# A new hand-written order of 914 operations, with new PSUM banks, in a one-core S4 mixer and MLP kernel

## The chip, the core and the metric

The kernel runs on one core of a Trainium2 chip. The metric is the device time of one execution in microseconds (us); lower is better. The engines are PE (TensorE, matrix multiplication), ACT (ScalarE), DVE (VectorE), POOL (GpSimd) and SP (SyncE, which here only issues transfers). "PEld" in the profile is PE's weight load.

## The reference

Two blocks with a residual each, over a sequence of 2048 rows of 512 channels in bfloat16:

```python
def A(u):                      # S4 convolution: N = 128 complex states for each channel
    dt = exp(log_dt)[:, None]
    logdA, dB = dt * (A_re + 1j * A_im), dt * (B_re + 1j * B_im)
    P = exp(logdA[:, :, None] * arange(L))
    K = einsum("dn,dnl,dn->dl", C_re + 1j * C_im, P, dB).real
    y = irfft(rfft(pad(u.T)) * rfft(pad(K)))[:, :L].T
    return y + u * Dskip
def B(x):                      # 512 -> 1376 -> 512
    return gelu(layernorm(x) @ w1 + b1) @ w2 + b2
h = x + A(layernorm(x))
out = h + B(layernorm(h))
```

The norms have no scale and no shift; the GELU is the tanh form. What a chip sees of part A is mostly the making of K (exponentials, sines, and chains of them), transforms written as matrix products, and the products of spectra.

## The kernel before

All work is recorded first, as 914 operations. `add(eng, cost, fn, r, w, new)` notes which engines may run an operation (one, or a choice of two), what it reads and writes, and which new PSUM tiles it opens. `Sched.run` then issues the operations strictly in the order of a list written out by hand:

```python
given = iter(SLOTS)
for k in ORDER:
    if k < 0:                    # a filler: four identity matmuls into bank -1-k, L1451
        ...
    o = ops[k // 2]
    o.e = o.eng[k % 2]           # which of its engines runs it
    for p in o.new:
        p.slot = int(next(given))  # which PSUM bank the tile takes
    order.append(o)
```

So an entry 2n is operation n on its first engine, 2n+1 the same operation on its second, and each engine gets its part of the list as its queue. `SLOTS` is a string of 196 digits, one bank of eight for each new PSUM tile. An engine never runs ahead of its own queue, and a matmul into a bank waits until what was there has been read.

The work in the order of time, with the lines in the profile of before:

- Kernel generation. Exponentials on ACT (L793), exponentials of the phases (L991, from matmuls at L988), then two chains of sines. The B chain has matmuls L1013/L1018, sines L1026 on ACT, multiplications L1036/L1043 on DVE. The A chain (chain1) has matmuls L1058/L1061, sines L1063 and multiplications L1068. It needs rows that go through DRAM (HL_d) and back. K is then made on PE (L1092), and its spectrum (L1120, L1145, L1166, L1187).
- Transforms of the normalised input: L946, L967, L971.
- The inverse, `inverse`, for two halves (b = 0, 1) and four chunks of channels. Each has two multiplications on DVE (L1235, 128x2048) or, for the last chunk, L1210, L689 and L1225; then matmuls (L1245), an evacuation of the bank, and a turn: on PE for one chunk (L1254), with a transposing transfer (L1261) for the others.
- `tail`: per quarter of the rows, matmuls L1315/L1319, the residual (L1322, or L1315 in the first), row statistics (L1323 and small DVE operations at L689 and L694), the normalised copy y2 (L1334 on DVE, L1336 on ACT), transposes on PE (L1346) in the first quarter and a transposing transfer in the others.
- `mlp`: for each quarter eleven groups of four matmuls (L1362) with a GELU on ACT (L1364), then matmuls L1378, the second residual L1380 on DVE, and stores.

`evac` copies a PSUM tile to SBUF, on ACT (L616) or on DVE (L618). `table` loads an activation table on ACT (L610). `dma` issues a transfer from SP or ACT (L632).

Of the kernel before, what the change touches and what calls it, by code (L numbers as in the profile page):

```python
# [275 lines left out]
class VS(V):  # L276
# [13 lines left out]
LAG = {"PE": 0.12, "ACT": 0.20, "DVE": 0.14, "POOL": 0.15, "SP": 0.15}  # L290
OWN = {"PE": 0.0, "ACT": 0.17, "DVE": 0.11, "POOL": 0.1, "SP": 0.0}
ORDER = [
# [35 lines left out]
]  # L328
SLOTS = "0124624620462046042642640426420206464620242002606204206242604026462064202064026406246024602406206420642016240364710404160364160743104523712460453347247364163210657000423751452706341725310671620547"


TURN = 450000
# [2 lines left out]
class Sched:  # L335
# [54 lines left out]
    def run(self, nslots):  # L390
# [13 lines left out]
        taken = [None] * nslots  # L404
        given = iter(SLOTS)
        order, seen = [], set()
# [1094 lines left out]
```

## Time and profile before

| | |
|---|---|
| median of three executions | 228.2 us (228.09 to 228.47) |
| profiled execution: span, first to last instruction | 226.4 us |
| granted TensorE clock, mean | 0.997 |
| PE busy | 198.1 us (87%), 2989 instructions |
| PE weight loads | 112.4 us (50%) |
| DVE busy | 174.3 us (77%) |
| ACT busy | 164.9 us (73%) |
| POOL busy | 13.8 us (6%) |

The profiled execution has no time of its own beside the span; the span lies 1.8 us below the median of the three. The shares are averages over stages with different limits, so they don't say what bounds a stage; the windows and the chain of waits do.

### The profile page before, as it was taken

Reading aid. Unit: us, or ns where it says so; the run is one execution under the profiler, and the core shown is the slowest. Engines: PE = TensorE matmul, PEld = TensorE weight load, DVE = VectorE, ACT = ScalarE, POOL = GpSimd, SP = SyncE. Lnnn points to the kernel's source line nnn. Section 1 sums busy time; section 2 is a strip of 40 time slices with the busy share of each in tenths; the row PEclk is TensorE's granted clock in tenths of the full one; section 3 lists DMA queues with packets and bytes.
Section 4 is the critical chain, followed back from the end, with each engine's and each line's share of the span. In section 5 each row is a group of like instructions: output and inputs, shape, how many; then the busy total and the mean of one; then the engine's idle time right before and its main releaser. Section 6 shows DMA issues by size and latency. Waiting matters only on the chain.

```text
span 226.4 us, 6876 instructions
## 1 busy us (share of the span) xinstructions
PE 198.1 (87%) x2989; PEld 112.4 (50%) x2989; DVE 174.3 (77%) x277; ACT 164.9 (73%) x205; POOL 13.8 (6%) x26
## 2 busy tenths in 40 slices
PE   6314977768999999999999868999999999999993
PEld 3102743234767478566576556644443444444552
DVE  7999789999998898889999999899827476013022
ACT  4999999999988998989999469695156206801900
POOL 2000301200010003000000010300000101000000
PEclk9999999999999999999999999999999999999998
DMA  5992074250003964657789495383050131313202
GB/s 152 179 189 74 7 243 128 50 146 6 6 3 75 130 174 135 163 143 213 163 176 280 136 306 110 108 191 90 0 127 0 32 88 46 72 44 78 75 23 70
DMA packets 43159, 25.09 MB, mean 111 GB/s; under 512 B 30197, under 2 KB 40697, under 8 KB 43130
## 3 DMA queue, kind: packets, MB, share of 16 engines
q1 hardware_dynamic: 42968, 24.59, 45.2%
q8 instruction: 23, 0.38, 0.7%
q10 hardware_dynamic: 162, 0.07, 0.1%
q14 instruction: 6, 0.05, 0.1%
HBM read 14.13 MB, written 5.28 MB: 86 GB/s over the span
## 4 chain that ended last, share of the span: by engine, by line
PE 65%; ACT 17%; DVE 11%; DMA 3%; issue 2%; POOL 0%; DVEq 0%; ACTq 0%; SPq 0%; POOLq 0%
PE ps L1378 17%; PE ps L1362 17%; PE ps L1092 8%; ACT ar L793 7%; PE ps L1245 6%; PE ps L946 4%; DVE ar L1235 4%; ACT ar L616 4%; PE ps L967 3%; ACT ar L1063 3%; ACT ar L991 3%; DVE ar L618 2%; DMA HL_d<-ar 2%; PE ps L1145 1%; PE ps L1061 1%
## 5 line engine op out<-in xcount | busy, mean ns | idle before, releaser
L616 ACT CAST ar<-ps 128x1024 bf16<-128x1024 f32 (+4 forms) x72 | 61.9, 903 | 14.0 <-PE ps L1245 9.2
L1364 ACT ACTIVATE ar<-ps,ar 128x512 bf16<-128x512 f32 (+1 forms) x44 | 27.0, 692 | 28.7 <-PE ps L1362 20.5
L1378 PE MATMUL ps<-ar 128*128 128x512 bf16 (+3 forms) x187 | 40.2, 367 | 0.0
L1362 PE MATMUL ps<-ar 128*128 128x512 bf16 (+1 forms) x176 | 39.8, 379 | 0.0
L1380 DVE TENSOR_TENSOR ar<-ps,ar 128x512 bf16<-128x512 f32 (+1 forms) x17 | 10.8, 655 | 28.3 <-PE ps L1378 28.3
L1378 PEld LDWEIGHTS <-ar 128*128 128x128 bf16 (+1 forms) x187 | 17.9, 98 | 19.7 <-issue 0.7
L1362 PEld LDWEIGHTS <-ar 128*128 128x128 bf16 (+1 forms) x176 | 17.3, 100 | 20.5 <-issue 0.8
L1235 DVE TENSOR_TENSOR ar<-ar 128x2048 bf16<-128x2048 bf16 x20 | 23.9, 1220 | 1.0 <-PE ps L1245 0.5
L1245 PE MATMUL ps<-ar 64*128 64x128 bf16 x672 | 21.7, 216 | 3.1 <-DVE ar L1235 2.1
L618 DVE CAST ar<-ps 128x1024 bf16<-128x1024 f32 (+3 forms) x19 | 21.3, 1129 | 3.3 <-PE ps L946 1.7
L1245 PEld LDWEIGHTS <-ar 64*128 64x128 bf16 x672 | 19.0, 94 | 7.8 <-DVE ar L1235 4.6
L1063 ACT ACTIVATE ar<-ps 128x1024 bf16<-128x1024 int16 x20 | 19.7, 1027 | 1.7 <-PE ps L1061 1.0
L1092 PE MATMUL ps<-ar 128*52 128x66 bf16 x512 | 19.4, 242 | 0.3 <-DVE ar L618 0.2
L1092 PEld LDWEIGHTS <-ar 128*52 128x52 bf16 x512 | 16.9, 130 | 4.4 <-issue 2.6
L689 POOL TENSOR_TENSOR ar<-ar 128x4 f32<-128x4 f32 (+1 forms) x6 | 8.6, 1436 | 141.7 <-DVE ar L694 99.5
L946 PE MATMUL ps<-ar 128*32 128x512 bf16 x256 | 15.9, 381 | 0.5 <-ACT ar L991 0.3
L793 ACT ACTIVATE ar<-ar 128x1024 bf16<-128x1024 f32 x16 | 15.7, 1045 | 0.6 <-DVE ar L788 0.6
L1026 ACT ACTIVATE ar<-ps 128x1024 bf16<-128x1024 int16 x16 | 15.7, 1033 | 0.3 <-PE ps L1018 0.2
L1068 DVE TENSOR_TENSOR ar<-ar 128x1024 bf16<-128x1024 bf16 x20 | 13.1, 685 | 1.2 <-ACT ar L1063 1.0
L967 PE MATMUL ps<-ar 128*64 128x512 bf16 (+2 forms) x160 | 14.0, 298 | 0.1
L1322 DVE TENSOR_TENSOR ar<-ps,ar 128x512 bf16<-128x512 f32 x12 | 8.0, 683 | 7.9 <-ACT ar L1364 4.3
L1061 PE MATMUL ps<-ar 128*32 128x256 f16 (+1 forms) x256 | 12.7, 301 | 1.2 <-ACT ar L1063 1.1
(85 smaller groups left out, 232.0 us busy)
## 6 DMA issues: line engine op xcount, KB each, us to landing
ar<-in_A_u_dram SPq DMA_DIRECT2D x16, 128.0 KB
ar<-in_A_u_dram SPq DMA_DIRECT2D x8, 256.0 KB
out_dram<-ar SPq DMA_DIRECT2D x30, 64.0 KB
ar<-in_B_w_dram SPq DMA_DIRECT2D x4, 344.0 KB
ar<-in_B_w_dram SPq DMA_DIRECT2D x2, 640.0 KB
AK_d<-ar SPq DMA_DIRECT2D x2, 512.0 KB
ar<-AK_d SPq DMA_DIRECT2D x2, 512.0 KB
AKc_d<-ar SPq DMA_DIRECT2D x4, 256.0 KB
```

What stands on the lines that cost most here:

```text
L616: act.copy(out_fn(), in_fn())
L618: dve.tensor_copy(out_fn(), in_fn())
L793: add("ACT", c_act(1024) + 0.03, lambda e, e0=e0: act.activation(free(EB0 // 2 + 4 * (16 - e0), [[8 * e0, 2], [4 * NB, NCH * CW // 4], [1, ...
L946: pe.matmul(pst(p)[32 * j:32 * j + 32, 512 * z:512 * z + 512], lhsT=BX.ap()[:, f0 + z, 16 - 16 * c:48 - 16 * c], rhs=src[2 * j + c].ap(), ...
L967: pe.matmul(pst(p)[64 * h:64 * h + 64, w * (k + r):w * (k + r) + w], lhsT=T.ap()[:, f, r, :], rhs=v[f:f + 1].ap()[:, 0, :], start=True, st ...
L1063: add("ACT", c_act(1024), lambda e, sc=sc: act.activation(sc.ap().rearrange("p z a b -> p (z a b)").rearrange("p (x a f) -> p a x f", a=4, ...
L1092: pe.matmul(o, lhsT=free(ta.lo // 2 + q * 4 * NP_ + f, [[4, NP_ + NA]]), rhs=free(tb.lo // 2 + q * 4 * NB + f, [[4, 2 * NB]]), start=ta is ...
L1235: dve.tensor_tensor(pq.ap().rearrange("p n d -> p (n d)"), a, b_, ALU.mult)
L1245: pe.matmul(pst(p)[:, 512 * h + 128 * k:512 * h + 128 * k + 128], lhsT=q.ap()[rows, x, :], rhs=TP[w].ap()[rows, f0 // 2 + k, :], start=(n ...
L1362: pe.matmul(pst(p)[:fs], lhsT=w1s[dc].ap()[:, fc * P:fc * P + fs], rhs=ybuf.ap().rearrange("p (t c) k -> p c t k", c=4)[:, dc], start=(dc ...
L1364: add("ACT", c_act(512, 1), lambda e, p=p, fc=fc, fs=fs: act.activation(hT.ap()[:fs, fc, :], pst(p)[:fs], ACT.Gelu_apprx_tanh, bias=b1_sb. ...
L1378: pe.matmul(pst(p)[:, c0:c1], lhsT=hT.ap()[:fs, fc, 128 * t:128 * t + 128], rhs=w2s[fc].ap()[:fs, c0:c1], start=(fc == 0), stop=(fc == NFC ...
```

## The change

Only the two tables at the top of the file differ. `ORDER` goes from 916 to 914 entries, `SLOTS` has the same length and other digits. The 914 operations are the same; 34 of them run on the other of their two engines. The list of before has two negative entries, -1 and -5, the fillers; the new one has none. The file gets one line longer, so that a line L1235 of before is L1236 after.

```diff
 ORDER = [
-    294, 0, 50, 2, 4, 62, 52, 154, 6, 64, 54, 8, 102, 12, 56, 66, 14, 10, 136,
+    58, 290, 0, 194, 2, 6, 52, 50, 8, 4, 54, 64, 62, 56, 10, 66, 68, 154, 102,
...
```

Three places show what the tables do. The first is ACT's queue after the table load for the sines, up to the first sine of the A chain (L1063, after L1064). L616 and L617 are evacuations. Before:

```order
L610 ACT_TABLE_LOAD
L701 ACTIVATE ar<-ar 128x512
L616 CAST ar<-ps 128x1024
L1026 ACTIVATE ar<-ps 128x1024 x6
L616 CAST ar<-ps 128x1024
L1026 ACTIVATE ar<-ps 128x1024 x2
L616 CAST ar<-ps 128x1024 x2
L1063 ACTIVATE ar<-ps 128x4x64x4 x10
```

And after:

```order
L611 ACT_TABLE_LOAD
L702 ACTIVATE ar<-ar 128x512
L1027 ACTIVATE ar<-ps 128x1024 x2
L617 CAST ar<-ps 128x1024
L1027 ACTIVATE ar<-ps 128x1024 x3
L617 CAST ar<-ps 128x1024
L1027 ACTIVATE ar<-ps 128x1024 x3
L617 CAST ar<-ps 128x1024 x3
L1064 ACTIVATE ar<-ps 128x4x64x4 x10
```

There are five evacuations among the eight sines of the B chain where there were four.

The second is DVE's queue in the first inverse chunks of the second half, where the statistics of the first quarter end (L694 behind L689) and the multiplications L1235 go on. Before:

```order
L694 SCALAR_TENSOR_TENSOR ar<-ar 128x4 x2
L1322 TENSOR_TENSOR ar<-ps,ar 128x512
L1235 TENSOR_TENSOR ar<-ar 128x2048
L694 SCALAR_TENSOR_TENSOR ar<-ar 128x4
L1235 TENSOR_TENSOR ar<-ar 128x2048
L1322 TENSOR_TENSOR ar<-ps,ar 128x512
L1323 BN_STATS ar<-ar 128x6
L1322 TENSOR_TENSOR ar<-ps,ar 128x512
L1235 TENSOR_TENSOR ar<-ar 128x2048 x2
```

And after:

```order
L690 TENSOR_TENSOR ar<-ar 128x4 x2
L695 SCALAR_TENSOR_TENSOR ar<-ar 128x4 x3
L1288 CAST ar<-ar 128x11
L1236 TENSOR_TENSOR ar<-ar 128x2048 x2
L695 SCALAR_TENSOR_TENSOR ar<-ar 128x4
L1323 TENSOR_TENSOR ar<-ps,ar 128x512
L1335 TENSOR_SCALAR ar<-ps,ar 128x512 x2
L1236 TENSOR_TENSOR ar<-ar 128x2048 x2
```

The last small operation of the statistics has moved behind the second of the two multiplications, and two scalings (L1335) have come from ACT.

The third is ACT's queue at the same place: the evacuation of an inverse tile is the one of form 128x128x8. Before:

```order
L616 CAST ar<-ps 128x128x8 x2
L1336 ACTIVATE ar<-ps,ar 128x512 x2
L616 CAST ar<-ps 128x512
L1336 ACTIVATE ar<-ps,ar 128x512
L616 CAST ar<-ps 128x512
L1336 ACTIVATE ar<-ps,ar 128x512
L616 COPY ar<-ps 128x512
L616 CAST ar<-ps 128x128x8
L616 COPY ar<-ps 128x512 x3
L616 CAST ar<-ps 128x512
L616 CAST ar<-ps 128x128x8
L610 ACT_TABLE_LOAD
```

And after:

```order
L617 CAST ar<-ps 128x4x2x128 x2
L611 ACT_TABLE_LOAD
L633 DMA ar<-in_A_u_dram 64x2048
L617 CAST ar<-ps 128x128x8
L633 DMA ar<-in_B_w_dram 128x1376 x2
L617 CAST ar<-ps 128x128x8
L1337 ACTIVATE ar<-ps,ar 128x512 x2
L617 CAST ar<-ps 128x512 x3
L617 COPY ar<-ps 128x512
L617 CAST ar<-ps 128x128x8
L617 COPY ar<-ps 128x512 x3
L633 DMA ar<-in_A_u_dram 64x2048
```

The table load for the GELU now stands ahead of the two 128x128x8 evacuations, four transfers that SP issued are issued here, two scalings are gone and the evacuations of 512 columns stand together ahead of the 128x128x8 one.

The other moves that a reader has to know, out of the 34 changes of engine: evacuations 239 and 383 of the transforms go from DVE to ACT and 389 from ACT to DVE (the first place); 233 and 241, ahead of L1120 and of the next L1120, go from DVE to ACT; 438, 463 and 466 go from DVE to ACT and 297, 300, 365 and 370 from ACT to DVE; the evacuation 510 of a turned tile goes from DVE to ACT; transfers 442, 479, 515, 517, 718 and 720 are issued by ACT and no longer by SP; a multiplication of the last chunk (697) is now some thirty operations earlier on DVE.

More of the change, by code (lines that the diff above doesn't have):

```diff
@@ L292 @@
 ORDER = [
[35 rows of a table removed]
[36 rows of a table added]
 ]
-SLOTS = "0124624620462046042642640426420206464620242002606204206242604026462064202064026406246024602406206420642016240364710404160364160743104523712460453347247364163210657000423751452706341725310671620547"
+SLOTS = "0731646240642646062424242420642004224066404662462426062400462064204626402640260246042604260246024602460230264301407644127314712531072462760513014235423170452374312767340403617410675301642056705627"
 TURN = 450000
```

71 rows, old and new, of the table ORDER are left out of this document.

## Prediction

> **What bounds the kernel now.** I read the windows first, cut where the chain of waits changes its character, then that chain, then the timelines of ACT, DVE and PE at the places where PE stands. The columns of the windows: the stretch in us from the span's start, its length, busy time of each engine (instructions), the granted TensorE clock, the share of the DMA engines, GB/s.
>
> ```profile
> core 0: us, PE busy (x) PEld busy (x) DVE busy (x) ACT busy (x) POOL busy (x), PEclk, DMA share, GB/s
> 0.00:31.00 31.00, 16.07 (x222) 10.24 (x222) 27.76 (x55) 27.90 (x32) 3.56 (x11) 1.00 0.61 135
> 31.00:56.90 25.90, 20.50 (x390) 8.95 (x386) 24.66 (x33) 25.26 (x28) 2.36 (x8) 1.00 0.35 95
> 56.90:121.30 64.40, 63.43 (x1536) 43.13 (x1536) 59.72 (x90) 59.83 (x71) 2.90 (x3) 1.00 0.58 132
> 121.30:138.40 17.10, 13.71 (x310) 9.63 (x308) 16.50 (x26) 11.99 (x16) 1.01 (x1) 1.00 0.71 202
> 138.40:222.90 84.50, 84.39 (x539) 40.46 (x539) 45.22 (x76) 39.87 (x62) 4.01 (x3) 1.00 0.31 74
> ```
>
> PE is the bound from 56.9 to 121.3 (0.97 us idle) and from 138.4 to 222.9 (0.11 us idle). Ahead of 56.9 ACT is it, with 27.90 of 31.00 and 25.26 of 25.90 us. From 121.3 to 138.4 it is DVE, 16.50 of 17.10, while PE stands for 3.39 us. So the change can act through three numbers: when the long PE stretch begins (56.89), when the last unbroken one begins (138.41), and whether either gets a hole. The chain of waits (start, us, what) says the same:
>
> ```profile
> 44.27 2.24 DMA ar<-HL_d
> ...
> 47.66 1.75 ACT ar L1063 x2
> ...
> 56.89 1.47 PE ps L1092 x40
> ...
> 71.18 1.22 DVE ar L618
> ...
> 72.56 1.96 PE ps L1120 x32
> ...
> 123.32 2.37 DVE ar L1235 x2
> ...
> 132.94 0.07 DVE ar L694
> 133.01 1.14 DVE ar L1235
> ...
> 136.07 2.29 DVE ar L1235 x2
> 138.41 1.96 PE ps L1245 x64
> ```
>
> **The change part by part.** *Fillers.* Both negative entries are gone, so PE issues eight matmuls and eight weight loads less. Timeline of PE:
>
> ```profile
> 12.95 0.40 PE L865 MATMUL ps<-ar 128*32 128x256 f16 x1 [5.09 <-DMA ar<-tab_I]
> ...
> 36.06 0.40 PE L1451 MATMUL ps<-ar 128*128 128x128 bf16 x4
> ...
> 43.49 0.38 PE L1451 MATMUL ps<-ar 128*128 128x128 bf16 x4 [0.43 <-ACT ar L616]
> ```
>
> That is 0.78 us of PE, in a stretch where PE is idle for 25.90 − 20.50 = 5.40 us and ACT sets the pace: gain 0. If ACT were not the cover, it would be 0.78 us at most. The lower bound is the clock: the row at 12.95 shows PE idle for 5.09 us, and the window 0 to 31 still has the clock at 1.00. [...]
>
> *Head, to 56.9.* ACT has, between the table load at 34.08 and the first sine of the second chain (L1063), twelve pieces of 1024 columns before (eight L1026, four evacuations) and thirteen after: evacuations 239 and 383 come from DVE, 389 goes to DVE. Timeline of ACT:
>
> ```profile
> 34.08 1.28 ACT L610 ACT_TABLE_LOAD   x1
> ...
> 45.25 1.92 ACT L616 CAST ar<-ps 128x1024 bf16<-128x1024 f32 x2
> 47.66 9.58 ACT L1063 ACTIVATE ar<-ps 128x1024 bf16<-128x1024 int16 x10 [0.48 <-PE ps L1061]
> ```
>
> One more piece takes 1.92/2 = 0.96; ACT waited 0.48 there for PE (which waited for the HL_d transfer), so the first sine moves by 0.96 − 0.48 = +0.5. Ahead of the table load the exponentials stand in another order, but their count is the same; the evacuation that leaves ACT for DVE there lets ACT start L991 no earlier than its input, so I keep 34.08. The ten sines stand behind one another in the same order, so L1092 starts at 57.4 in place of 56.89. Upper end: the whole 0.96, if the transfer is late too. Lower end: 0, since the HL_d transfer alone reached 46.51 (44.27 + 2.24).
>
> *Middle, 56.9 to 121.3.* The same PE work in another order, so only the 0.97 us of idle can change. The evacuation of 1.22 us in the chain at 71.18 (233) goes from DVE to ACT, as does 241; ACT has the cheaper one:
>
> ```profile
> L616 ACT CAST ar<-ps 128x1024 bf16<-128x1024 f32 x47 | 46.0, 1022 | 13.1 <-PE ps L1245 9.2 <-PE ps L967 1.2 <-issue 1.1
> ...
> L618 DVE CAST ar<-ps 128x1024 bf16<-128x1024 f32 x14 | 16.9, 1218 | 2.0 <-PE ps L946 1.7 <-PE ps L1120 0.3
> ```
>
> 0.2 us is the difference, and DVE is no longer asked for it there. With the other small waits I take −0.5: half of the idle, which gives back the head's delay. Ends: −0.97 (no idle left) and +1.0 (as much idle again, which the swaps in the other direction, 438, 463, 466 from DVE to ACT and 370, 365, 297, 300 from ACT to DVE, could make). Moved transfers: 479 and 442 now are issued by ACT, some 0.5 us each, where ACT has 64.40 − 59.83 = 4.57 us to spare; cover gone, they cost 1.0.
>
> *The hole, 121.3 to 138.4.* Here I find the loss. Timelines of DVE, ACT and PE:
>
> ```profile
> 122.19 0.68 DVE L618 COPY ar<-ps 128x1024 bf16<-128x1024 bf16 x1
> 123.32 2.36 DVE L1235 TENSOR_TENSOR ar<-ar 128x2048 bf16<-128x2048 bf16 x2 [0.45 <-PE ps L1245]
> ...
> 132.86 0.15 DVE L694 SCALAR_TENSOR_TENSOR ar<-ar 128x4 f32<-128x4 f32 x1
> ...
> 134.07 0.69 DVE L1322 TENSOR_TENSOR ar<-ps,ar 128x512 bf16<-128x512 f32 x1
> 134.79 0.69 DVE L1323 BATCH_NORM_STATS2 ar<-ar 128x6 f32<-128x512 bf16 x1
> ...
> 127.74 1.01 ACT L616 CAST ar<-ps 128x1024 bf16<-128x1024 f32 x1 [1.47 <-PE ps L1245]
> ...
> 132.05 1.01 ACT L616 CAST ar<-ps 128x1024 bf16<-128x1024 f32 x1 [3.29 <-PE ps L1245]
> 133.05 1.45 ACT L1336 ACTIVATE ar<-ps,ar 128x512 bf16<-128x512 f32 x2
> 134.39 0.58 ACT L616 CAST ar<-ps 128x512 bf16<-128x512 f32 x1
> ...
> 137.14 1.06 ACT L616 CAST ar<-ps 128x1024 bf16<-128x1024 f32 x1
> ...
> 141.48 1.28 ACT L610 ACT_TABLE_LOAD   x1
> 143.10 1.27 ACT L1364 ACTIVATE ar<-ps,ar 128x512 bf16<-128x512 f32 x2 [0.34 <-PE ps L1362]
> ...
> 138.41 1.96 PE L1245 MATMUL ps<-ar 64*128 64x128 bf16 x64 [0.69 <-DVE ar L1235]
> ```
>
> On DVE the copy at 122.19 (0.68) goes to ACT, and a multiplication of the last chunk (697, 1.2) takes its place and the wait of 0.45 behind it: 0.68 + 0.45 − 1.2 = +0.1. Ahead of the last two L1235 stand two scalings (540, 548; some 0.6 each, as other 512-column operations from PSUM) and no longer the L1322 at 134.07 and the L1323 at 134.79, some 0.6 each: 0. So DVE alone would reach 138.41 at +0.1.
>
> ACT has the loss. The last operation of the row statistics (539, at 132.86) stood between two L1235 and now stands behind both: 1.14, and 0.1 for a small cast put in there. So ACT's two scalings, which wait for it, start at 133.05 + 1.14 + 0.1 + 0.1 (DVE's own delay) = 134.4. Behind them ACT has two scalings (1.45), three evacuations of 512 columns (0.58 each by the row at 134.39; estimated 0.55 as one begins before the other ends) and a copy of the same size before evacuation 686, the one at 137.14 (1.06), which frees the PSUM bank of the matmuls at 138.41: 134.4 + 1.45 + 4 × 0.55 + 1.06 = 139.1. Before, 686 ended at 138.20 and DVE at 138.36. So the unbroken stretch starts at 139.15: +0.75. Ends: +0.1 (686 hidden, DVE decides) and +1.3 (the whole 1.24 of the statistics is passed on). The table load (1.28, with the 0.34 behind it) moves to ahead of the evacuation at 127.74, with a transfer's issue (718, 0.5) behind it: 2.1 us, against a wait of 1.47; 0.65 is left, and the 3.29 of waiting behind it hides that. Issues 515 and 517 (1.0) go into those 3.29 too. If nothing hid them, the upper end grows by 0.65.
>
> [...]
>
> *From the start of that stretch to the end.* Same PE work, 84.4 us, same order of halves; the last half-tile, its L1380 and its store stay last. Term 0. What gets tighter is the transposing transfer (L1261) whose result L1319 reads:
>
> ```profile
> 163.36 0.62 PE L1245 MATMUL ps<-ar 64*128 64x128 bf16 x16
> ...
> 165.23 5.34 PE L1362 MATMUL ps<-ar 128*128 128x512 bf16 x24
> 170.50 0.84 PE L1319 MATMUL ps<-ar 128*64 128x512 bf16 x6
> ...
> 165.06 1.60 SPq L1261 DMA_TRANSPOSE ar<-ar  x1
> ```
>
> From the end of L1245 (163.98) to L1319 (170.50) PE had 6.5 us of other work; now six groups of four L1362 stand between, 5.3 by the row of 24. Ends: 0 and +1.2, if all 6.5 were needed.
>
> **Sum.** 0 (fillers) + 0.5 (head) − 0.5 (middle) + 0.75 (hole) + 0 = +0.75, on a span of 226.4; the runs' median is 228.2, 1.8 above the span, and I add the change to the median: 228.95, told as 229.0. A difference of 0.2% (0.46 us) is about what a measurement of this kernel can tell from none.
>
> **Rivals.**
> 1. Faster. The swaps take the middle's idle away wholly (−0.97), the head's +0.5 doesn't appear because the HL_d transfer is the later one, and in the hole DVE decides (+0.1): 228.2 − 0.87 = 227.3. For it: the wait at 71.18 is on the chain and its evacuation got cheaper. Against it: PE has just 0.97 to give there, and 686 stands behind more of ACT's work. It decides if 686 ends before DVE's last L1235. 0.25.
> 2. No change. Middle and hole cancel (−0.5 of idle removed, head hidden, hole +0.5): 228.2. For it: PE is full for 149 of 226 us. 0.17.
> 3. More slower. The transfer at 165.06 lands late for L1319, +1.2 on the forecast's +0.75: 230.2. For it: the shorter cover. Against it: the issue ends at 166.66, 3.8 us ahead of use. 0.12.
> 4. Clock falls without the fillers. The L1092 at 56.89 would run its first 1.47 us at half speed, +1.5: 228.2 + 0.75 + 1.5 = 230.4. Against it: clock 1.00 after 5.09 us idle. 0.03.
>
> **How the numbers follow.** The forecast (about +0.5 to +1.3, 228.7 to 229.5) has 0.43. Slower: 0.43 + 0.12 + 0.03 = 0.58; same 0.17; faster 0.25. The range leaves out less than 2 in 10: down to 227.3, where the first rival ends, and up to 230.6, the sum with the hole's upper end (1.3), the head unabsorbed (0.5) and half of the third rival (0.6).
>
> **What would show it.** Head: the first L1063 at 48.1 and the first L1092 at 57.4. Middle: the L1245 at 121.39 within half a us. Hole: the scaling on ACT starting near 134.4, its 1024-column evacuation near 138.0, and the unbroken PE stretch at 139.15. Last stretch: PE idle under 0.3 us after that. I am wrong if PE's idle between 57 and 121 is not between 0.3 and 1.5, if the hole's length falls, or if a wait on a transfer or a bank opens behind 139.

## The result, and the profile after

The changed kernel takes 232.12 us (median of six, 230.03 to 234.16) beside 228.43 for the kernel before on the same chip. The ratio is 1.0122, with a 95% interval of 1.0081 to 1.0164: slower, by 2.8 us where 0.75 was forecast, and the median lies outside the range. A later series of ten gave 232.34 (228.83 to 234.00), ratio 1.0082 [1.0039, 1.0125]. The ratios leave out executions more than 1.5% above the fastest of their kernel, here one of the six (the profiled one) and five of the ten; the medians of all executions differ by 1.6 to 1.7%. The profiled execution is the slowest of the six, 234.16, with a span of 232.4. A profile of the later series (run e6 below) took 232.23; it shows the second of the two waits that follow, longer, and not the first.

The page: PE's busy time and the granted clock in 40 slices. Work is the same but for the eight filler matmuls, the idle grew, and one slice past the middle has a lower clock (the last slice lies behind PE's work).

```profile
PE 196.5 (85%) x2975; PEld 114.1 (49%) x2981; DVE 175.7 (76%) x281; ACT 162.8 (70%) x201; POOL 13.7 (6%) x26
...
PEclk9999999999999999999997999999999999999998
```

The windows, cut at the same events as before (first L1093, first L1246 of the second half's inverse, the start of PE's last unbroken stretch, its end):

```profile
56.82:126.50 69.68, 64.12 (x1538) 44.53 (x1538) 61.56 (x93) 58.97 (x69) 2.90 (x3) 0.99 0.59 132
126.50:144.83 18.33, 14.12 (x308) 10.47 (x309) 15.13 (x24) 12.67 (x17) 1.93 (x1) 0.95 0.71 187
144.83:228.70 83.87, 83.28 (x534) 40.91 (x539) 46.09 (x79) 38.07 (x59) 3.02 (x3) 1.00 0.30 66
```

The head ends at 56.82 (56.89 before). The middle is 69.68 long in place of 64.4, so PE stood for 5.6 us in place of 0.97. The next stretch is 18.33 in place of 17.1. The last is 0.6 shorter. The chain of waits says what the middle waited for, and it is transfers (start, us, what):

```profile
104.66 4.39 DMA AKc_d<-ar
...
109.98 5.03 DMA ar<-AKc_d
...
115.06 1.07 PE ps L968 x20
...
118.00 4.71 DMA ar<-ar
...
124.80 1.77 PE ps L1255 x16
```

SP issues them, and the timeline of its queue shows the reason. After (first block) and before (second), with SP's own longest wait for this write between them (us in total, times, longest):

```profile
97.94 0.41 SPq L633 DMA_DIRECT2D AL_d<-ar  x1
98.58 0.38 SPq L633 DMA_DIRECT2D AKc_d<-ar  x1
103.83 0.78 SPq L633 DMA_DIRECT2D ar<-AL_d  x1
104.66 0.46 SPq L633 DMA_DIRECT2D AKc_d<-ar  x1
...
109.12 0.34 SPq L633 DMA_DIRECT2D ar<-AKc_d  x1
...
109.98 0.43 SPq L633 DMA_DIRECT2D ar<-AKc_d  x1
110.50 4.36 SPq L1262 DMA_TRANSPOSE ar<-ar  x1
...
118.00 1.56 SPq L1262 DMA_TRANSPOSE ar<-ar  x1
...
121.36 2.84 SPq L1262 DMA_TRANSPOSE ar<-ar  x1
```

```profile
SPq L633 <- DMA AL_d<-ar: 5.9, 2, 4.7
```

```profile
96.09 2.94 SPq L632 DMA_DIRECT2D AKc_d<-ar  x2
...
104.35 0.33 SPq L632 DMA_DIRECT2D ar<-AKc_d  x1
...
106.58 2.04 SPq L1261 DMA_TRANSPOSE ar<-ar  x1
...
111.80 2.03 SPq L1261 DMA_TRANSPOSE ar<-ar  x1
...
117.30 1.58 SPq L1261 DMA_TRANSPOSE ar<-ar  x1
```

After: the load at 103.83 (operation 662) reads what the write at 97.94 (478) puts into DRAM, and SP stands for 4.7 us until that has landed. Behind it waits a write (464) that before went out at 98.67 and now goes out at 104.66. Two loads need it, the first at 109.12 when it has landed. The three transposing transfers of the first half's inverse (486, 493 and 500) stand behind them and are issued at 110.50, 118.00 and 121.36, not at 106.58, 111.80 and 117.30. The first of them also holds SP for 4.36 us, 2.04 before. PE then waits twice (timeline of PE; the row of ACT is what the second wait goes back to, the last row is before's, for the length of the same matmuls):

```profile
115.06 1.07 PE L968 MATMUL ps<-ar 128*64 128x128 bf16 x20 [1.96 <-DMA ar<-AKc_d]
...
122.81 2.84 ACT L617 CAST ar<-ps 128x1024 bf16<-128x1024 f32 x3 [2.75 <-DMA ar<-ar]
...
123.88 0.42 PE L1188 MATMUL ps<-ar 18*64 18x256 bf16 x14 [1.65 <-ACT ar L617]
...
126.50 2.84 PE L1246 MATMUL ps<-ar 64*128 64x128 bf16 x64
...
121.32 1.96 PE L1245 MATMUL ps<-ar 64*128 64x128 bf16 x64
```

The second wait is ACT's: its evacuation could not overwrite the buffer that the late transfer (118.00, 4.71 us) was still reading. The slower matmuls are a consequence of their own: these 64 took 1.96 before and take 2.84, because the clock was halved:

```profile
121.56:124.97 3.41, 1.25 (x23) 0.43 (x20) 3.41 (x5) 2.16 (x3) 0.00 (x0) 1.00 1.20 253
124.97:128.38 3.41, 3.41 (x52) 3.21 (x51) 0.62 (x2) 3.32 (x4) 0.00 (x0) 0.50 0.87 250
```

In a stretch of 3.41 us PE was busy for 1.25; in the next 3.41 us the clock is 0.50.

In the profile of e6 the waits come out otherwise. SP stands for a shorter time (662 is issued at 102.57, 464 at 103.40), and PE has no wait before L968. The transposing transfers are still issued late, at 108.57, 116.53 and 120.47, and the second wait alone makes the loss (SP, PE):

```profile
108.57 4.25 SPq L1262 DMA_TRANSPOSE ar<-ar  x1
...
116.53 2.58 SPq L1262 DMA_TRANSPOSE ar<-ar  x1
...
122.39 0.42 PE L1188 MATMUL ps<-ar 18*64 18x256 bf16 x14 [2.23 <-ACT ar L617]
```

### The profile page after: what moved, and what is told of

The parts are those of the page before. It is cut to its first block, busy times and chain, and to the rows that moved or that the text cites. A ratio compares the mean times of both kernels' runs of the same rounds, so it can differ in the third digit from the quotient of the medians.

```text
span 232.4 us, 6858 instructions
## 1 busy us (share of the span) xinstructions
PE 196.5 (85%) x2975; PEld 114.1 (49%) x2981; DVE 175.7 (76%) x281; ACT 162.8 (70%) x201; POOL 13.7 (6%) x26
## 4 chain that ended last, share of the span: by engine, by line
PE 52%; ACT 17%; DVE 15%; DMA 8%; issue 5%; SPq 2%; POOL 0%; DVEq 0%; ACTq 0%; POOLq 0%
PE ps L1363 15%; PE ps L1379 13%; PE ps L1093 6%; PE ps L1246 5%; ACT ar L617 4%; ACT ar L1064 4%; ACT ar L992 4%; DMA ar<-ar 4%; ACT ar L1027 3%; PE ps L968 3%; DVE ar L1236 2%; DMA ar<-AKc_d 2%; PE ps L947 2%; DMA AKc_d<-ar 2%; DVE ar L619 2%
## 5 line engine op out<-in xcount | busy, mean ns | idle before, releaser
L617 ACT CAST ar<-ps 128x1024 bf16<-128x1024 f32 (+3 forms) x69 | 59.6, 927 | 20.2 <-PE ps L1246 6.0
L1365 ACT ACTIVATE ar<-ps,ar 128x512 bf16<-128x512 f32 (+1 forms) x44 | 27.6, 687 | 30.9 <-PE ps L1363 30.9
L1363 PE MATMUL ps<-ar 128*128 128x512 bf16 (+1 forms) x176 | 40.1, 379 | 0.3 <-DMA ar<-ar 0.3
L1379 PE MATMUL ps<-ar 128*128 128x512 bf16 (+2 forms) x182 | 39.3, 366 | 0.3
L1363 PEld LDWEIGHTS <-ar 128*128 128x128 bf16 (+1 forms) x176 | 17.2, 100 | 20.8 <-DMA ar<-ar 0.8
L1236 DVE TENSOR_TENSOR ar<-ar 128x2048 bf16<-128x2048 bf16 x20 | 23.8, 1217 | 4.5 <-PE ps L1246 4.0
L619 DVE CAST ar<-ps 128x1024 bf16<-128x1024 f32 (+4 forms) x22 | 23.2, 1064 | 4.4 <-PE ps L947 2.0
L1246 PE MATMUL ps<-ar 64*128 64x128 bf16 x672 | 21.9, 221 | 3.6 <-DVE ar L1236 2.0
L1246 PEld LDWEIGHTS <-ar 64*128 64x128 bf16 x672 | 19.7, 97 | 7.8 <-DVE ar L1236 5.6
L1064 ACT ACTIVATE ar<-ps 128x1024 bf16<-128x1024 int16 x20 | 19.7, 1048 | 1.8 <-PE ps L1062 0.9
L1093 PE MATMUL ps<-ar 128*52 128x66 bf16 x512 | 19.0, 243 | 0.4 <-DVE ar L1069 0.4
L1093 PEld LDWEIGHTS <-ar 128*52 128x52 bf16 x512 | 17.0, 130 | 3.9 <-issue 2.0
L968 PE MATMUL ps<-ar 128*64 128x512 bf16 (+2 forms) x160 | 13.8, 298 | 3.2 <-DMA ar<-AKc_d 2.0
L690 DVE TENSOR_TENSOR ar<-ar 128x512 f32<-128x512 f32 (+3 forms) x24 | 12.2, 515 | 0.5
```

The lines of the kernel that those rows point to most:

```text
L617: act.copy(out_fn(), in_fn())
L619: dve.tensor_copy(out_fn(), in_fn())
L968: pe.matmul(pst(p)[64 * h:64 * h + 64, w * (k + r):w * (k + r) + w], lhsT=T.ap()[:, f, r, :], rhs=v[f:f + 1].ap()[:, 0, :], start=True, st ...
L1064: add("ACT", c_act(1024), lambda e, sc=sc: act.activation(sc.ap().rearrange("p z a b -> p (z a b)").rearrange("p (x a f) -> p a x f", a=4, ...
L1093: pe.matmul(o, lhsT=free(ta.lo // 2 + q * 4 * NP_ + f, [[4, NP_ + NA]]), rhs=free(tb.lo // 2 + q * 4 * NB + f, [[4, 2 * NB]]), start=ta is ...
L1236: dve.tensor_tensor(pq.ap().rearrange("p n d -> p (n d)"), a, b_, ALU.mult)
```

## The experiments

Two theories stood against the forecast's: the order on SP's queue makes transfers late ("queue"), and PE's thin stretches halve the clock ("gate"); the rival to both was that the missing fillers are the loss. Diffs show entries of the order (2n or 2n+1 is operation n). The ratio is to the kernel before, run beside them. A mean clock of 0.993 or less is counted as at least one window at half clock, an estimate from the one above (0.5 × 3.41 of some 230 us is 0.0074; the profile of before, with half clock only from 224.96 on, behind PE's work, has 0.997). It doesn't say where the window lies: five executions of e10 have means of 0.966 to 0.968, as much as four windows would take off, and took 228.01 to 228.69, no longer than the others. No profile shows where that half clock lies.

**One write moved (e1).**

```diff
-    885, 827, 750, 1324, 1260,
+    885, 827, 750, 928, 1324, 1260,
...
-    1318, 1270, 816, 928, 1274,
+    1318, 1270, 816, 1274,
```

> The changed kernel with one transfer moved: the write of a spectrum's second half (464, AKc_d<-ar) is issued by SP ahead of the load 662 (ar<-AL_d) and not behind it. Queue theory (in the changed kernel 662 waits until 103.8 for another write to land, 464 behind it is issued at 104.66 in place of 98.67, so the loads 470 and 469 that need it and the transposing transfers 486, 493, 500 come 4 to 6 us later): 464 at about 99, PE's wait of 2.0 us before L968 at 115 gone, the wait of ACT for the transposing transfer at 118 to 122.7 gone or under 1 us, granted clock 1.00 from 120 to 130; 228.5 to 229.7 us against some 231 for the changed kernel. Filler theory (the lost time is half clock for want of fillers): no change, 230 to 233. Forecast's theory (late statistics in the stretch of the second half's first inverse chunks, +0.75): no change from this edit.

Measured: 230.76 us (228.82 to 232.55), ratio 1.0061 [1.0030, 1.0092]. The wait before L968 is gone, but the transposing transfers are issued at 108.21, 114.85 and 118.31, still late by 1 to 3 us, and PE waits again, later:

```profile
121.18 0.42 PE L1188 MATMUL ps<-ar 18*64 18x256 bf16 x14 [1.20 <-ACT ar L617]
```

A window at half clock follows at 123.08 (the clock is 0.81 from 120 to 125 and 0.85 from 125 to 130, and the 64 L1246 at 123.10 take 3.56). So this write is a part of the cause; the rest counts too. The first transposing transfer is not held by the queue here: SP was free from 106.59 and waited until 108.21 for the evacuation that it reads, and e5 and e10 issue it at 108.24 and 108.17, so 1.6 us of its lateness comes from the new compute order. The second one is: four loads stand ahead of it, and SP is free only at 114.75. The time lies above what I expected.

**A load ahead of the write in the kernel before (e2).**

```diff
-    934, 933, 1260, 928,
+    934, 933, 1260, 958, 1324, 928,
```

> The kernel before with two transfers moved: the write 479 and the load 662 that waits for it stand on SP ahead of the write 464. Queue theory: SP stands for some 4 us at 662, 464 goes out near 102 to 104 in place of 98.67, the transposing transfers come some 4 us later, and PE gets a hole between 112 and 126: slower by 1 to 4 us, 229.5 to 232. Filler theory: the fillers are kept, so within 0.5 us of before. If the order of these three is not the cause, within 0.5 us of before too.

Measured: 228.50 (228.03 to 229.62), ratio 0.9998 [0.9969, 1.0026]: no loss. Here 479 is the later of the two writes that 662 reads, where in the changed kernel it is 478. It was issued at 96.63 and had landed by 98.86, so SP stood for 1.7 us and not for 4.9, and the transposing transfers came within 0.4 us of before. One pair alone does not make the loss.

**The fillers: put back (e3), taken from before (e4).**

```diff
-    298, 446, 302,
+    298, 446, -7, 302,
...
-    332, 344,
+    332, -5, 344,
```

> The changed kernel with the two fillers put back at the same operations of PE as before (four identity matmuls ahead of 151 and four ahead of 172), in banks that are free there. Queue theory: as the changed kernel, 230 to 233, with the same waits at 115 and 118 to 123. Filler theory: back to 228.2 to 229, with the clock at 1.00 between 120 and 130.

Measured: 229.98 (228.57 to 231.68), ratio 1.0060 [1.0034, 1.0086]. Not back to before, and 8 of 12 executions still had a window at half clock; but nearer to it than the changed kernel in its own series, on another chip, with intervals that overlap. In the one profile (229.03) the writes landed sooner and PE had no wait before L968, as in e6 without fillers. Its window at half clock lies in the head, from 38.68 to 42.09 (the clock is 0.93 from 31 to 57), with the fillers in place, and the first L1093 comes at 57.73. So the fillers aren't shown to help here.

```diff
-    256, -1, 490,
+    256, 490,
...
-    308, -5, 270,
+    308, 270,
```

> The kernel before without its two fillers, nothing else. Forecast's theory (the fillers stand where ACT sets the pace): within 0.3 us of before, first L1092 at 56.9. Filler theory: one more window at half clock in most executions, 0.5 to 2 us slower.

Measured: 229.39 (228.33 to 230.91), ratio 1.0024 [0.9994, 1.0054], inconclusive as a ratio; but 11 of 12 executions had a window at half clock, against 8 of 27 of the kernel before beside them (33 of 86 over three series). In the profile one of two starts at 47.43 behind a window with 1.48 us of PE, and the first L1092 comes at 57.96 and not at 56.89:

```profile
44.02:47.43 3.41, 1.48 (x28) 0.69 (x29) 3.41 (x5) 3.07 (x4) 0.00 (x0) 1.00 0.25 57
47.43:50.84 3.41, 3.15 (x48) 1.63 (x40) 3.01 (x4) 2.27 (x3) 0.00 (x0) 0.50 0.54 176
```

So the fillers make such windows rarer in the order of before. They don't keep them out: the profile of e9 below, with them and with this head, has one at 47.33 (eight L1061 take 0.65 us at 47.88, and 0.39 at 48.09 in before). In the changed order without them the clock from 31 to 57 is 1.00 in the profiles of after, e1 and e5, and the first L1093 came at 56.8 to 57.0.

**The transfers of the middle in the order of before (e5).** 718 and 720 stay on ACT.

```diff
-operations on SP: ..., 478, 468, 662, 464, 511, 470, 516, 469, 486, 663, 514, 661, 660, 493, ...
+operations on SP: ..., 478, 651, 440, 464, 442, 468, 441, 479, 511, 470, 661, 99, 486, 469, 662, 660, 493, ...
```

> The changed kernel with all transfers of SP and ACT between about 82 and 140 us (40 of them, from the writes of the first spectrum up to the second half's second transposing transfer) on SP and in the order of before; the compute engines' orders stay the new ones. Queue theory: the middle is repaired wholly, 228.3 to 229.5, the L1246 at the start of the second half's inverse near 121.4, and what is left over before is the forecast's +0.75 in the stretch 121 to 139 or less. If the compute order itself costs the time, 230 or more.

Measured: 229.95 (229.85 to 230.71), ratio 1.0065 [1.0040, 1.0089]. The spread is gone: 0.86 us in place of 4 to 5. What is left is one wait of 1.15 before L968 for 469, and a window at half clock (0.50 from 135.83 to 139.24), behind one with 1.60 us of PE:

```profile
132.42:135.83 3.41, 1.60 (x52) 1.34 (x46) 3.34 (x11) 1.01 (x1) 1.93 (x1) 1.00 1.08 287
```

All six executions had a clock of 0.990 or less, three of them 0.963. So the old order of the transfers is not by itself the repair: with the new compute order 0.65% is left.

**The changed kernel again (e6).** Unaltered.

> The changed kernel once more, unaltered, beside the others. Queue and gate theory together (loss = waits for late transposing transfers, 0 to 4 us and different from execution to execution, plus one window of 3.4 us at half clock in the stretch of the second half's first inverse chunks, 1.3 us): 229.5 to 233, every execution at a clock of 0.993 or less, and PE's last unbroken stretch 83.4 long against 84.4 before. If the first 6 executions were chance: 228.5 to 229.5.

Measured: 232.34 (228.83 to 234.00). Seven of ten had a clock of 0.993 or less, not all ten as expected; the three others took 228.83, 229.11 and 231.68. PE's last stretch is 83.38 long (143.32 to 226.70). So the first series was no accident, and the loss differs from execution to execution.

**Fillers where PE waits (e8).** On e5:

```diff
-    1362,
+    -6, -6, 1362,
...
-    1370,
+    -6, -6, 1370,
```

> The changed kernel with all transfers in the order of before (as in the earlier run with that edit alone, 229.95), and 16 identity matmuls as fillers: eight ahead of the matmuls of 681 and eight ahead of those of 685, where PE waited 0.92 and 1.46 us. Gate theory (PE's waits in that stretch make a window of too little work, and the clock is halved for the 3.41 us behind it): no window at half clock between 120 and 145, the stretch from 672 to 690 some 17.5 in place of 18.8 long, 228.5 to 229.2. If the half clock comes from elsewhere: 229.8 to 230.5, the fillers costing up to 0.6.

Measured: 229.52 (228.81 to 231.68), ratio 1.0045 [1.0024, 1.0066]. Eleven of twelve executions kept a mean clock of 0.996 or more, where none had. The stretch from 672 to 690 is 17.54 long (122.56 to 140.10), against 18.76 in e5. That is what the gate theory expected. The time is above the 229.2 that I expected at most, since the wait for 469 stayed (1.07), and the gain over e5 lies within the intervals.

**One load more (e10).** On e8, 469 ahead of the transposing transfer 486.

```diff
-    972, 938,
+    938, 972,
```

> The changed kernel with the transfers in the order of before and 16 filler matmuls in the inverse stretch (229.5 in its own run), and the load 469 (ar<-AKc_d) issued ahead of the transposing transfer 486. Queue theory (469 went out at 109.99 because 486 ahead of it waited for ACT's evacuation until 108.24; PE then waited 1.07 us for it): 469 near 105, that wait gone, start of L1255 near 120.5 in place of 121.56, 228.3 to 228.6. If the middle is late because of the compute order itself: 229.2 to 229.7.

Measured: 228.51 (228.01 to 229.40), ratio 1.0002 [0.9985, 1.0020]. L1255 starts at 120.33, before at 120.32. The loss is gone, with the changed compute order and the changed banks still in place, apart from the sixteen fillers. The profiled execution, 229.40, has a wait of PE of 1.48 us at 142.33 that the profile puts to nothing it shows.

**The changed transfers in the kernel before (e12).**

```diff
-operations on SP: ..., 464, 442, 468, 441, 479, 511, 470, 661, 486, 469, 662, 660, 493, ...
+operations on SP: ..., 441, 653, 478, 468, 662, 464, 511, 470, 516, 469, 486, 663, 514, 661, 660, 493, ...
+operations on ACT: 442, 479, 515, 517
```

> The kernel before with the transfers of SP between 82 and 140 us in the changed kernel's order, and with 442, 479, 515 and 517 issued by ACT as there; compute order and fillers as before. Queue theory: the transposing transfers 486, 493 and 500 come later than 106.6, 111.8 and 117.3 by 1 to 5 us, waits of PE between 112 and 126, a wide spread of times, median 229.5 to 232. If the compute order is needed for the loss: within 0.5 us of before, as the run with 479 and 662 moved alone.

Measured: 230.95 (229.42 to 232.88), ratio 1.0095 [1.0054, 1.0136]. That is about the loss of the change, with the compute order, banks and fillers of before. The place where SP stands is another one: the write 468 waits until 100.64 for its evacuations, as it did before (100.63), and now holds 464 behind it until 102.02; 662 costs next to nothing. The transposing transfers are issued at 107.44, 113.75 and 117.31, so the second is 2 us late, and the third not at all. ACT waited again for a late transposing transfer (timeline of ACT), and six of seven executions had a window at half clock:

```profile
119.30 2.84 ACT L616 CAST ar<-ps 128x1024 bf16<-128x1024 f32 x3 [1.10 <-DMA ar<-ar]
```

**Statistics back in their place (e11).** On e10, operations 537 and 539.

```diff
-    1366, 1368, 1074, 1078,
+    1074, 1366, 1078, 1368,
```

> As the kernel with 469 ahead of 486, and the end of the first quarter's statistics put back to where before had it: 537 on POOL ahead of the multiplication 683, 539 on DVE between 683 and 684. Forecast's theory (the scalings and evacuations on ACT up to 686 wait for 539, and 686 sets the start of 690): the stretch from 672 to 690 17.1 in place of 17.5 long, another 0.3 to 0.5 us less than the run with 469 alone, 227.8 to 228.2. If 686 is late for another reason: no difference to that run.

Measured: 229.72 (228.78 to 231.96), ratio 1.0036 [1.0004, 1.0068]: a miss, slower than e10. The small operation 539 waits for POOL, and now DVE stands for it, ahead of a multiplication that PE waits for (timelines of DVE, POOL and ACT; the last row is POOL's in the kernel before):

```profile
134.34 0.16 DVE L695 SCALAR_TENSOR_TENSOR ar<-ar 128x4 f32<-128x4 f32 x1 [0.90 <-POOL ar L690]
...
132.38 1.93 POOL L690 TENSOR_TENSOR ar<-ar 128x4 f32<-128x4 f32 x1 [42.00 <-DVE ar L1288]
...
134.54 1.45 ACT L1337 ACTIVATE ar<-ps,ar 128x512 bf16<-128x512 f32 x2 [0.76 <-DVE ar L695]
...
131.25 1.01 POOL L689 TENSOR_TENSOR ar<-ar 128x4 f32<-128x4 f32 x1 [41.30 <-DVE ar L694]
```

PE fell into a window at half clock at 135.68 (56 of L1246 took 3.17, where 64 took 1.96 at 130.43) and the stretch became 19.91 long. Being late there had hidden POOL's time: ACT's scalings start at 134.54, where e10 with 539 behind both multiplications has 134.56.

**The changed tail on before (e7, e9).** The first cut is at 690, the second behind 616.

```diff
-order of before
+order of before up to the cut, then the changed kernel's order of what is left
```

> The kernel before up to the matmuls of operation 690 (start of PE's last unbroken stretch), and from there the changed kernel's order (banks: the changed kernel's, renamed so that they fit). Batching theory (in the changed kernel the 64-row matmuls L1319 and L1245 stand together, 4 changes into them in place of 10, and the unbroken stretch is 1.0 us shorter): 227.2 to 227.6, faster by 0.3 to 0.45%. If the shorter stretch comes from something done earlier, ahead of 690: 228.0 to 228.6. If the tail's transfers come late in the new order (third rival): 229 or more.

Measured: 230.67 (229.73 to 231.58), ratio 1.0092 [1.0059, 1.0124]. The seam made waits: 86.0 us for the last stretch, with these in it.

```profile
141.95 2.75 PE L1362 MATMUL ps<-ar 128*128 128x512 bf16 x12 [1.74 <-ACT ar L616]
165.07 5.34 PE L1362 MATMUL ps<-ar 128*128 128x512 bf16 x24 [0.93 <-DVE ar L618]
```

86.0 − 1.74 − 0.93 = 83.3, so without these two waits the stretch would be 1.1 shorter there as well.

> The kernel before up to the last matmuls of the second quarter's first MLP part (PE's operation 616), and from there the changed kernel's order, so that the first inverse stretch and the GELU's start stay as before and the eight L1319 groups stand together. Batching theory: PE's last unbroken stretch 0.5 to 0.8 us shorter than 84.4, no new wait of more than 0.3, 227.5 to 227.9. If batching buys nothing: 228.2 to 228.5. If the seam makes waits as in the earlier cut: over 229.

Measured: 228.41 (228.12 to 231.36), ratio 1.0003 [0.9983, 1.0023], no difference: in the profile (its slowest execution, 231.36) a wait of 0.78 for DVE's L1380 took the gain (84.35 in place of 84.42). The shorter stretch is thus seen in profiles of the changed kernel (83.87, and 83.38 in e6) and not shown in a time. No version beat the kernel before.

## Why the prediction was wrong

**The step that failed is the middle.** It said that "only the 0.97 us of idle can change" and took −0.5, with ends of −0.97 and +1.0. It was +5.2 in the profile (L1246 at 126.56 in the chain, 121.39 before) and +3.8 in that of e6. I walked PE, ACT and DVE and priced the two transfers that moved to ACT at 0.5 us of ACT each. I did not walk SP's own queue, where a load (662) had been moved ahead of a write (464). What the runs show in its place is a path through SP: transfers that are issued late because of what stands ahead of them, then a wait of ACT and PE for them, then half clock. The end of +1.0 was no bound: it came from what PE had idle before, while a queue that stands for 5 us puts that on everything behind it. The range's upper end left even this +1.0 out. e10 and e12 show this step from both sides: the changed compute order and banks with repaired transfers and fillers in the inverse stretch cost nothing, and the changed transfers on the old compute order cost 0.95%. They don't show that one pair of transfers is the cause: where SP stands differs between the changed kernel (662) and e12 (468), and with the old transfers alone (e5) 0.65% was left.

**The fourth rival was priced for the wrong place.** It had a window at half clock at the first L1092 for want of fillers, at 0.03. No run shows this term: in after the clock is 1.00 there, and without the fillers in the old order (e4) the first forty L1092 take 1.47 us, as in before. The half speed itself is in the records, elsewhere: a window at half clock came in 13 of the 16 executions of the changed kernel by their mean clock, at 123 to 125 in the two profiles (after: 0.50 from 124.97; e6: L1255 at 123.31 takes 1.89 for 1.07), behind the wait for the transfers. My argument against this rival was also misread. The column showed 1.00 around the idle of 5.09 us because the trace has no clock record ahead of 26.98 us in that execution. Matmuls of one form before and after that time (timeline of PE, kernel before):

```profile
18.67 1.86 PE L865 MATMUL ps<-ar 128*32 128x256 f16 x29 [0.35 <-DVE ar L694]
...
71.55 0.83 PE L1061 MATMUL ps<-ar 128*32 128x256 f16 x24
```

64 ns each against 35: the head may well have run at half clock, and the row was no evidence either way. Nor did PE stand for the whole 3.41 us ahead of the dips that the windows show: it was busy there for 1.25 to 1.60 us, as the last section has it.

**The hole came out nearly in size where it can be seen alone, but with a cause that isn't shown.** The forecast had ACT's scalings at 134.4, its 1024-column evacuation at 138.0, PE's last stretch at 139.15. In e10, where the middle is repaired (ACT, ACT, PE):

```profile
134.56 1.44 ACT L1337 ACTIVATE ar<-ps,ar 128x512 bf16<-128x512 f32 x2 [0.91 <-DVE ar L695]
...
137.79 1.06 ACT L617 CAST ar<-ps 128x1024 bf16<-128x1024 f32 x1
...
138.91 1.94 PE L1246 MATMUL ps<-ar 64*128 64x128 bf16 x63 [0.51 <-ACT ar L617]
```

PE is released by the evacuation, not by DVE as before, at +0.5 against the +0.75 taken, though with fillers in the stretch. So ACT's part of the walk holds. What starts it doesn't: the forecast put the scalings at 134.4 because 539 stands behind both multiplications, and e11 puts it back between them and finds the scalings at 134.54. POOL's operation, which 539 reads, ends at 134.31 there and at 132.26 before; it begins 1.1 later and takes 0.92 longer. The forecast had no term for POOL, and that its 1.24 came to the same start is luck. (Its sum for DVE, 0.68 + 0.45 − 1.2, gives −0.07 as written; the delay meant is +0.07.) In the changed kernel itself the stretch is longer by 1.2, of which the half clock is most: 1.88 us of it lie in that window, which is 0.94 lost.

**The head** was taken at +0.5 and measured −0.07: L1064 begins at 47.38 in the chain, before at 47.66, because the table load came 0.27 earlier (33.81 against 34.08), and the thirteenth piece went into the wait that ACT had before: from the first piece to the first L1064 it is 11.74 for thirteen, and 11.75 for twelve with the wait. **The fillers** cost nothing to remove in the head of the changed profiles, as said, but the reason given leaves out what they do: by e4 windows at half clock come more often without them in the old order. **The last stretch** was taken at 0 and is 0.6 to 1.0 shorter. In before PE changes eight times into a group of L1245 or L1319, with 64-column or 64-row tiles; in the new order three times. That these changes are what costs the time is argued, not shown: the tail's order differs in other ways too. **The third rival** did not happen: no L1320 waited for its transposing transfer, and the one wait of PE on a transfer in the last stretch is 0.28 us, before L1363 at 189.13. The transfers that came late were those of the first half, 50 us earlier.

The whole in the profile of e6, against before: L1246 at 125.13 for 121.32 is +3.81, the stretch to 690 +1.10 (18.19 for 17.09), the last stretch −1.04 (83.38 for 84.42), the end +0.12; together +3.99, and the spans differ by 230.4 − 226.4 = 4.0.

## What to carry to other kernels

Where an order is rewritten, walk the queue of the engine that only issues transfers as closely as the compute engines: a load that waits for a write to land held the transfers behind it here (662 for 4.7 us, so that 464 went out at 104.66, before at 98.67), and those belong to other stages. An idle bound from the profile of before limits gains, not losses. A wait of 2 us cost nearly 4 where slower matmuls came behind it: in e6 the wait of 2.23 was followed by 1.55 us more in two groups of them (L1255 1.89 for 1.07, L1246 2.69 for 1.96). In after the clock behind the wait of 1.65 was 0.50 for 3.41 us. So look at PE's busy share around a new wait before it is called small.

## What the runs showed of the hardware

The dip in the profile of after is a clock of 0.50 for 3.41 us, from 124.97 to 128.38. It starts 102.40 us, thirty times 3.41, behind the first clock record of that trace, at 22.57. The windows from 47.43 in e4 and from 135.83 in e5, of the same length, have 0.50 too. In the 3.41 us ahead of these three PE was busy for 1.25 (37%), 1.48 (43%) and 1.60 us (47%); by the timelines of PE it was 1.06 in e11, 1.64 in e9 and 1.71 in e1. Behind a window of 1.68 us (49%; after, from 111.31) the clock stayed at 1.00, so the share of busy time is not the whole of it. In before and after, cut from the first record on, all other windows up to the last stretch have 59% or more and full clock behind them. In e5 the longest wait of PE that ended in that window was 1.46 us. Two windows with more of PE, of before and e8, with no dip behind them (before has 1.00 from 132.79 to 136.20, and e8's mean clock is 1.000):

```profile
129.38:132.79 3.41, 2.15 (x58) 1.78 (x58) 3.32 (x9) 0.74 (x1) 1.01 (x1) 1.00 0.96 211
```

```profile
131.80:135.21 3.41, 1.96 (x66) 1.88 (x61) 3.34 (x10) 1.01 (x1) 1.77 (x1) 1.00 1.14 280
```

The clock records begin at 22.57 us in after and at 26.98 in before. If the dips keep to such a start in every execution, that may be one reason, an untested one, for times that differ between executions of one program: the kernel before took 228.28 in the median of 53 executions with a mean clock above 0.995, and 229.36 in the median of the other 33. The time from a write's issue to its landing also varied: 5.8 us for the write of 72 KB to AL_d at 97.94 and 4.4 for that of 256 KB to AKc_d at 104.66 in after, and 2.2 at most for the write to AL_d at 96.63 in e2; what it depends on was not tried.
